# The last output tile in three pieces with its other terms summed ahead: a parallel attention and gated-MLP block

## The chip, the core and the metric

The kernel runs on one core of one Trainium2 chip. The metric is the device time of one execution in microseconds, as the median of several runs. The core has five engines with queues of their own: TensorE (PE) for matrix products, VectorE (DVE), ScalarE (ACT), GpSimd (POOL), and SyncE (SP), which here mostly issues DMAs. TensorE writes into PSUM, which VectorE and ScalarE read; DMAs move data between SBUF and the chip's memory. An engine works through its queue in order, and engines wait for each other by semaphores.

## What is computed

One block on a sequence of 2048 rows with 512 columns, in bfloat16. With `xn` the layer-normed input, the output is the residual plus two branches, both of which end in a matrix product:

```python
x = A_x                                   # (1, 2048, 512)
xn = _layernorm(x, axis=-1)
return x + _A_ref(xn, A_wqkv, A_wo) + _B_ref(xn, B_w_in, B_w_sp, B_b_sp, B_w_out)

# _A_ref: 32 heads of 16, each row attends to 8 rows behind it, 2 apart
#   o = softmax(q.k / 4) v ;  return o @ wo                   # (512 x 512)
# _B_ref: z = gelu(xn @ w_in);  z1, z2 = halves of 688
#   g = w_sp @ layernorm(z2) + b_sp                           # mixes the rows
#   return (z1 * g) @ w_out                                   # (688 x 512)
```

The "gated features" of the title are `z1 * g`; "the other part" is the attention branch and the last 48 of the 688 gated features.

## The kernel before, in words

The 2048 rows are 16 tiles of 128. Everything is written as named operations: `op_(name, after, f)` (line 149) stores a function and the names that must be issued before it. Five lists written out by hand (lines 569 to 616) give the order of the names on TensorE, ScalarE, VectorE, GpSimd and SyncE. `advance` (line 623) walks them, TensorE's list first, and issues what an operation needs ahead of it. The names in `after` only set the order of issue; the waits on the chip are added by the framework from the tiles that instructions read and write, and the traces show them per tile: who reads a PSUM tile waits for the last write that was issued into it, in whichever part of the tile.

The work goes through these stages: norm, transposes and the input products (lines 164 to 340), local attention on VectorE, the row mixing on TensorE (`mix`, line 467), the gate `z1 * g` on VectorE and its transposition by DMA into `uT` (line 474), and the output stage, which is where the change lies.

The output stage (lines 507 to 566) works on four groups of four tiles. Group n has tiles {0, 2, 4, 6}, {1, 3, 5, 7}, {8, 10, 12, 14} and {9, 11, 13, 15}. Each output tile (128 rows, 512 float32 columns) fills one PSUM bank. There are eight banks in five PSUM tiles: `mm[0]`, `mm[1]`, `mm[2]` with two banks each, `aux[0]`, `aux[1]` with one. Groups 0 and 2 use the first four entries of `banks` (lines 507 and 508), groups 1 and 3 the last four. Into each bank three products are summed:

- `gated_full` (line 512): 640 of the 688 gated features, five matmuls of 512 columns (`MF` is 5);
- `gated_rest` (line 517): the last 48 features, one matmul;
- `attention_out` (line 523): 64 narrow matmuls for the four tiles of a group side by side, one quarter of the array's rows each.

TensorE's list ends with `gf2 re2 re3 ao2 ao3` and then the full products of group 3, tile by tile. Group 3 thus has its short and its attention products first (`re3`, `ao3`), and its gated products last: tiles 9, 13 and 11 whole (`gf3.9`, `gf3.13`, `gf3.11`), tile 15 in two halves of 256 columns (`gfl0`, `gfl1`), both in the one bank `aux[1]`.

What follows a finished tile: for groups 0 and 1, ScalarE copies the bank (`E`, line 554) and VectorE adds the residual `xr` (`F`, line 555); for groups 2 and 3 VectorE adds the residual straight from PSUM (`F`, line 560) and writes bfloat16. SyncE stores the tile (`S`, line 561). Tile 15 has two adds of 256 columns (`Fl0`, `Fl1`, line 565) and two stores of 64 KB (`Sl0` from SyncE, `Sl1` from ScalarE, line 566). The residual `xr[1]` is loaded long before (`R1`, line 504).

`stmp` (line 85) is a float32 SBUF tile of 128 x 4 x 256 that the softmax uses (lines 394 to 404) and nothing after it. Line 664 is the end of the program: the last waits for all DMAs and the engines' closing handshake stand under it.

Of the kernel before, what the change touches and what calls it, by code (L numbers as in the profile page):

```python
# [10 lines left out]
ALU = mybir.AluOpType  # L11
PSUM = bass.MemoryType.PSUM

P = 128
S = 2048
D = 512
NT = S // P
C = D // P
DH = 16
# [8 lines left out]
F = 2 * FH  # L28
FHALF = FH // 2
MF = FH // P  # L30
# [12 lines left out]
def kernel(  # L43
# [13 lines left out]
    V = nc.vector  # L57
    A = nc.scalar
    G = nc.gpsimd
    PE = nc.tensor  # L60
    SP = nc.sync

    x2 = A_x.rearrange("b s d -> (b s) d")
    out2 = out.rearrange("b s d -> (b s) d")
# [20 lines left out]
    stmp = sb.tile([P, 4, GS], F32, name="stmp")  # L85
# [8 lines left out]
    wout = wts[:, DH * D:(DH + MF + 1) * D].rearrange("p (m n) -> p m n", m=MF + 1)  # L94
# [5 lines left out]
    uT = [r[:, 0:(MF + 1) * HS].rearrange("p (m s) -> p m s", m=MF + 1) for r in qk_r]  # L100
# [17 lines left out]
    xr = [wsp_r[n].rearrange("p (i d) -> p i d", i=8) for n in (2, 0)]  # L118
# [7 lines left out]
    mm = [ps.tile([P, 2, D], F32, name=f"mm{n}") for n in range(3)]  # L126
    aux = [ps.tile([P, D], F32, name=f"aux{n}") for n in range(2)]
# [21 lines left out]
    def op_(name, after, f):  # L149
        assert name not in do, name  # L150
        do[name], needs[name] = f, list(after)
# [146 lines left out]
    for i in range(NT):  # L298
        g = i // 4 * 4
# [73 lines left out]
    for c, th in BUF:  # L373
        n = f"{c}{th}"
# [128 lines left out]
    for th in range(2):  # L503
# [1 line left out]
            xr[th], x2[th * HS:(th + 1) * HS, :].rearrange("(i p) d -> p i d", p=P)))  # L505

    banks = [mm[0][:, 0, :], mm[0][:, 1, :], mm[1][:, 0, :], mm[1][:, 1, :],
             mm[2][:, 0, :], aux[0][:], mm[2][:, 1, :], aux[1][:]]
    groups = [[8 * th + 2 * g + t for g in range(4)] for th in range(2) for t in range(2)]
    po = {i: banks[4 * (n % 2) + g] for n, tiles in enumerate(groups) for g, i in enumerate(tiles)}  # L510

    def gated_full(i, start, stop, c=slice(0, D)):
        th, t0 = i // 8, (i % 8) * P
        for m in range(MF):
            PE.matmul(po[i][:, c], uT[th][:, m, t0:t0 + P], wout[:, m, c], start=(start and m == 0), stop=(stop and m == MF - 1))  # L515
# [7 lines left out]
    def attention_out(n, start, stop):  # L523
        th, s = n // 2, n % 2
        for d in range(DH):
            for g in range(4):
                PE.matmul(po[groups[n][g]], op[32 * g:32 * g + 32, th, d, s * P:(s + 1) * P], wo_r[32 * g:32 * g + 32, d, :],  # L527
                          start=(start and d == 0), stop=(stop and d == DH - 1), tile_position=(32 * g, 0))

    U = [[f"U{j}" for j in range(8 * th, 8 * th + 8)] for th in range(2)]  # L530
    EVM = [f"G{j}" for j in range(NT)] + ["Bc", "Tc4"]
    for n in (0, 1):
        op_(f"gf{n}", LO + U[0] + EVM, lambda n=n: [gated_full(i, True, False) for i in groups[n]])
        op_(f"re{n}", [f"gf{n}"], lambda n=n: gated_rest(groups[n], False, False))
        op_(f"ao{n}", [f"re{n}", "a0.11"], lambda n=n: attention_out(n, False, True))
    op_("gf2", U[1] + [f"E{i}" for i in groups[0]], lambda: [gated_full(i, True, False) for i in groups[2]])
    op_("re2", ["gf2"], lambda: gated_rest(groups[2], False, False))
    op_("re3", U[1] + [f"E{i}" for i in groups[1]], lambda: gated_rest(groups[3], True, False))
    op_("ao2", ["re2", "a1.11"], lambda: attention_out(2, False, True))
    op_("ao3", ["re3", "a1.11"], lambda: attention_out(3, False, False))  # L540
    halves = [slice(0, D // 2), slice(D // 2, D)]
    tail = [groups[3][g] for g in (0, 2, 1, 3)]
    for i in tail[:3]:
        op_(f"gf3.{i}", ["ao3"], lambda i=i: gated_full(i, False, True))
    for n, c in enumerate(halves):
        op_(f"gfl{n}", ["ao3"], lambda n=n, c=c: gated_full(groups[3][3], False, n == 1, c))

    def o_of(i):
        return ot[i]
# [10 lines left out]
                    lambda i=i: V.tensor_tensor(o_of(i), po[i], xr[1][:, i % 8, :], ALU.add))  # L560
            op_(f"S{i}", [f"F{i}"], lambda i=i: SP.dma_start(out2[i * P:(i + 1) * P, :], o_of(i)))

    for n, c in enumerate(halves):
        i = groups[3][3]
        op_(f"Fl{n}", [f"gfl{n}", "R1"], lambda c=c: V.tensor_tensor(o_of(i)[:, c], po[i][:, c], xr[1][:, i % 8, c], ALU.add))  # L565
        op_(f"Sl{n}", [f"Fl{n}"], lambda n=n, c=c: (SP, A)[n].dma_start(out2[i * P:(i + 1) * P, c], o_of(i)[:, c]))


    pe = """wu T0a T0 B wd z0a T1 z0b T2 z1 T3 z2 T4 z3 T5 z4 T6 z5 T7 z6 z7 y0 y1 z8 z9 z10 z11 z12 z13 z14
        k0 k1 q0 q1 z15 k2 k3 q2 q3 k4 k5 q4 q5 k6 k7 q6 q7  # L570
        v0 v1 v2 v3 v4 v5 v6 v7 y2 y3 y4 y5 y6 y7 y8 y9 y10 y11 y12 y13 y14 y15
        M0 M1 M2 M3 M4 M5 M6 M7 M8 M9 M10 M11 M12 M13 M14 M15
        gf0 gf1 re0 re1 ao0 ao1 gf2 re2 re3 ao2 ao3""".split() + [f"gf3.{i}" for i in tail[:3]] + ["gfl0", "gfl1"]
    for n in pe:
        a, x = n[0], n[1:]
        if n in do:
# [26 lines left out]
    dve = """b0 ag0 b1 ag1 n0a n0 b2 ag2 n1 b3 n2 ag3 b4 ag4 n3 b5 ag5 n4 b6 ag6 b7 n5""".split()  # L603
    for i in range(6, NT):
# [2 lines left out]
        m00 f00 p00 m01 zs8 m10 zb8 zs12 m11 p01 zb12 m20 p10 m21 p11 m30 p20 m31 p21 p30 X0 p31 HW u0 X1 C0 g0 a0.0 u1 a0.1 C1 g1 g2  # L607
        a0.2 g3 a0.3 g4 a0.4 g5 a0.5 a0.6 g6 a0.7 g7 a0.8 a0.9 g8 a0.10 a0.11 g9 g10 a1.0 a1.1 g11 a1.2 g12 a1.3 g13
        a1.4 g14 a1.5 a1.6 g15 a1.7 a1.8 a1.9 a1.10 a1.11""".split()
    OUT = [i for n in range(3) for i in groups[n]] + tail[:3]  # L610
    dve += [f"F{i}" for i in OUT] + ["Fl0", "Fl1"]
    pool = ["b16"] + [f"gr{i}" for i in range(NT)] + "zr0 zr4 f01 zr8 kh2 f10 zr12 kh3 f11 f20 f21 f30 f31".split()
    sp = """x0 x1 x2 x3 x4 x5 x6 x8 wy x12 wk wq wv t8 t9 t10 t11 t12 t13 t14 t15 W0 kh0 W1 kh1 vh
        W2 W3 LO0 LO1 W4 U0 W5 LO2 LO3 U1 U2 W6 LO4 U3 U4 W7 U5 U6 U7 U8 U9 U10 R0 U11 U12 U13 R1 U14 U15""".split()
    sp += [f"S{i}" for i in OUT] + ["Sl0"]
    act.append("Sl1")
    lists = [pe, act, dve, pool, sp]
    assert sorted(sum(lists, [])) == sorted(do), (set(do) ^ set(sum(lists, [])))
# [50 lines left out]
```

## Time and profile before

| | |
|---|---|
| runs | 200.99, 201.28, 201.07 us; median 201.07 |
| the profiled execution | 200.92 us |
| its span, first to last instruction | 199.1 us |
| granted TensorE clock | 1.0 |
| stores to the output | 15 of 128 KB and 2 of 64 KB |
| last matmul ends | 195.77 us in the span |
| last store issued | 196.58 us in the span |

All times inside an execution are counted from the start of the span. In the views, L515 is line 515 of the kernel; PE is TensorE's matmuls, PEld its weight loads, SPq and ACTq the DMA issues of SyncE and ScalarE. In a group's row, `out<-in` are the tiles, then come partitions x columns and types, the count, the busy time in us and the mean duration in ns, and then the idle time of the engine before it and who ended it. In the timeline a row that ends in x3 is three instructions run together: start of the first, time from there to the end of the last. A matmul's duration includes its way through the array, so durations of matmuls that follow each other overlap; adds of VectorE overlap by a little too.

### The profile page before, as it was taken

Reading aid. Unit: us, or ns where it says so; the run is one execution under the profiler, and the core shown is the slowest. Engines: PE = TensorE matmul, PEld = TensorE weight load, DVE = VectorE, ACT = ScalarE, POOL = GpSimd, SP = SyncE. Lnnn points to the kernel's source line nnn. Section 1 sums busy time; section 2 is a strip of 40 time slices with the busy share of each in tenths; the row PEclk is TensorE's granted clock in tenths of the full one; section 3 lists DMA queues with packets and bytes.
Section 4 is the critical chain, followed back from the end, with each engine's and each line's share of the span. In section 5 each row is a group of like instructions: output and inputs, shape, how many; then the busy total and the mean of one; then the engine's idle time right before and its main releaser. Section 6 shows DMA issues by size and latency. Waiting matters only on the chain.

```text
span 199.1 us, 4537 instructions
## 1 busy us (share of the span) xinstructions
PE 194.8 (98%) x1939; PEld 122.7 (62%) x1939; DVE 177.7 (89%) x203; ACT 89.8 (45%) x130; POOL 38.8 (19%) x67
## 2 busy tenths in 40 slices
PE   8999999999999999999999999999999999999993
PEld 2566666667777766666666666666666654443441
DVE  5999896899898999989999999999999999996234
ACT  2587898796559996671562211112211110043000
POOL 5577122002999330330000000000000000000000
PEclk9999999999999999999999999999999999999999
DMA  6999566910987999998199999999993569904133
GB/s 163 361 360 205 95 142 131 206 17 0 197 140 142 194 189 142 184 182 156 40 220 214 184 155 239 253 112 255 212 212 69 112 206 232 191 3 159 55 105 105
DMA packets 68452, 32.58 MB, mean 164 GB/s; under 512 B 56912, under 2 KB 66512, under 8 KB 68304
## 3 DMA queue, kind: packets, MB, share of 16 engines
q1 hardware_dynamic: 65568, 24.12, 58.8%
q0 software_dynamic: 2176, 7.40, 20.1%
q10 hardware_dynamic: 688, 0.77, 1.3%
q8 instruction: 15, 0.25, 0.5%
q14 instruction: 5, 0.04, 0.1%
HBM read 10.03 MB, written 2.10 MB: 61 GB/s over the span
## 4 chain that ended last, share of the span: by engine, by line
PE 94%; DMA 2%; DVE 1%; POOL 0%; SPq 0%; issue 0%; DVEq 0%
PE mm L471 37%; PE mm L321 21%; PE mm L230 18%; PE mm L527 7%; PE mm L515 7%; PE aux L515 2%; DMA z<-in_A_x_dram 2%; PE mm L520 1%; PE aux L212 1%; SPq L162 0%; DVE stats L169 0%; POOL rstd L176 0%; DVE z L565 0%; DVE z L179 0%; DVEq L664 0%
## 5 line engine op out<-in xcount | busy, mean ns | idle before, releaser
L471 PE MATMUL mm<-z,wsp 128*128 128x344 bf16 x512 | 74.8, 309 | 0.0
L471 PEld LDWEIGHTS <-wsp 128*128 128x128 bf16 x512 | 50.1, 98 | 24.6
L321 PE MATMUL mm<-xnT,wts 128*32 128x512 bf16 x768 | 41.9, 380 | 0.0
L230 PE MATMUL mm<-wts,xnT 128*128 128x344 bf16 x256 | 39.0, 309 | 0.0
L321 PEld LDWEIGHTS <-wts 128*32 128x32 bf16 x768 | 29.5, 140 | 12.0 <-issue 0.6
L422 DVE TENSOR_TENSOR prod<-vp,a_sb 128x4096 bf16<-128x4096 bf16 x16 | 36.1, 2285 | 0.0
L485 ACT ACTIVATE qk<-mm,b_col 128x688 bf16<-128x688 f32 x16 | 13.3, 831 | 46.0 <-PE mm L471 41.1
L230 PEld LDWEIGHTS <-xnT 128*128 128x128 bf16 x256 | 24.6, 98 | 12.1 <-issue 0.8
L355 DVE TENSOR_TENSOR prod<-qk 128x4096 bf16<-128x4096 bf16 x12 | 26.9, 2287 | 1.4 <-DMA qk<-qk 1.2
L426 DVE TENSOR_TENSOR prod<-prod,prod 128x8192 bf16<-128x8192 bf16 x6 | 26.5, 4420 | 0.0
L334 ACT CAST qk<-mm 128x1024 bf16<-128x1024 f32 x16 | 16.2, 1012 | 7.8 <-PE mm L321 7.8
L310 ACT ACTIVATE z<-mm 128x688 bf16<-128x688 f32 x16 | 11.8, 748 | 5.7 <-PE mm L230 5.3
L363 POOL DMA_DIRECT2D prod<-prod x10 | 8.7, 1022 | 27.9 <-DVE zvar L279 15.6
L527 PE MATMUL mm<-wts,xnT 32*128 32x512 bf16 x192 | 14.2, 374 | 0.0
L515 PEld LDWEIGHTS <-qk 128*128 128x128 bf16 x85 | 8.2, 98 | 9.4 <-issue 0.8
L515 PE MATMUL mm<-wts,qk 128*128 128x512 bf16 x60 | 13.6, 379 | 0.0
L247 ACT ACTIVATE z<-mm 128x688 bf16<-128x688 f32 x16 | 11.8, 744 | 1.8 <-PE mm L230 1.8
L169 DVE BATCH_NORM_STATS2 stats<-z 128x6 f32<-128x512 bf16 x16 | 10.7, 671 | 1.5 <-DMA z<-in_A_x_dram 1.4
L560 DVE TENSOR_TENSOR z<-mm,wsp 128x512 bf16<-128x512 f32 x6 | 3.8, 684 | 8.5 <-PE mm L527 5.2
L527 PEld LDWEIGHTS <-xnT 32*128 32x128 bf16 x256 | 6.4, 93 | 7.7 <-issue 0.8
L554 ACT CAST z<-mm 128x512 bf16<-128x512 f32 x6 | 3.2, 598 | 13.7 <-PE mm L527 12.3
L176 POOL TENSOR_TENSOR rstd<-rstd,mhalf 128x1 f32<-128x1 f32 x16 | 9.0, 561 | 1.3
(82 smaller groups left out, 170.2 us busy)
## 6 DMA issues: line engine op xcount, KB each, us to landing
prod<-prod POOLq DMA_DIRECT2D x10, 512.0 KB, 7.4
wts<-in_A_wo_dram SPq DMA_DIRECT2D x4, 512.0 KB, 6.6
wsp<-in_A_x_dram SPq DMA_DIRECT2D x2, 1024.0 KB, 6.0
out_dram<-z SPq DMA_DIRECT2D x15, 128.0 KB, 1.8
wts<-in_A_wqkv_dram SPq DMA_DIRECT2D x3, 512.0 KB, 8.6
z<-in_A_x_dram SPq DMA_DIRECT2D x2, 512.0 KB, 6.2
wsp<-z POOLq DMA_DIRECT2D x2, 512.0 KB, 6.4
wsp<-wts POOLq DMA_DIRECT2D x2, 512.0 KB, 8.8
```

The source lines that it names most:

```text
L230: PE.matmul(t[:, hh, 0:FHALF], xnT[:, kc, i * P:(i + 1) * P], w_z[part][:, kc, hh * FHALF:(hh + 1) * FHALF], start=(kc == 0), stop=(kc == ...
L247: A.activation(z2[:, i, :].rearrange("p (a b) -> p a b", a=2), t[:, :, 0:FHALF], ACT.Gelu_apprx_tanh, **total)
L310: op_(f"yg{i}", [f"y{i}"], lambda: A.activation(z1u[:, i, 0:FH].rearrange("p (a b) -> p a b", a=2), t[:, :, 0:FHALF], ACT.Gelu_apprx_tanh))
L321: PE.matmul(t[32 * g:32 * g + 32, dd, :], w, r, start=(kc == 0), stop=(kc == C - 1), tile_position=(0, 32 * g))
L334: op_(f"{a}c{p}", [f"{a}{p}"], lambda: A.copy(home(a, p), t[:].rearrange("p d (t s) -> p d t s", t=2)))
L355: V.tensor_tensor(pr, q, k, ALU.mult)
L422: return lambda: V.tensor_tensor(dst, vp[:, :, th, off:off + GS], a_sb[:, th, W - 1 - w].unsqueeze(1).broadcast_to([P, DH, GS]), ALU.mult)
L426: return lambda: V.tensor_tensor(dst, dst, x, ALU.add)
L471: PE.matmul(t[:, hh, 0:FHALF], w[:, k, (j % 2) * P:(j % 2 + 1) * P], z2[:, k, hh * FHALF:(hh + 1) * FHALF], start=(k == 0), stop=(k == NT ...
L485: lambda: A.activation(gs[j % 3].rearrange("p (a b) -> p a b", a=2), t[:, :, 0:FHALF], ACT.Identity, bias=b_col[:, j:j + 1]))
L515: PE.matmul(po[i][:, c], uT[th][:, m, t0:t0 + P], wout[:, m, c], start=(start and m == 0), stop=(stop and m == MF - 1))
L527: PE.matmul(po[groups[n][g]], op[32 * g:32 * g + 32, th, d, s * P:(s + 1) * P], wo_r[32 * g:32 * g + 32, d, :], start=(start and d == 0), ...
```

## The change

The last output tile, 15, no longer gathers all its terms in one bank.

- **Banks.** The last two entries of `banks` trade places: tiles 13 and 15 (and 5 and 7) trade `mm[2]`'s second half and `aux[1]`. Tile 15's short and attention products are now in `mm[2]`'s second bank; its accumulation ends with `ao3` (the `stop` flag).
- **Order.** Group 3's full products go 9, 11, 13 where they went 9, 13, 11.
- **The early sum.** `Fe`, a new VectorE add ahead of tile 9's, sums that bank and the residual into `early`, a float32 view of the first two quarters of `stmp`.
- **Three pieces.** Tile 15's gated product goes into three other banks: columns 0 to 255 into `mm[0]`, 256 to 383 into `mm[1]`, 384 to 511 into `aux[0]` (`last_full`: five matmuls each). `aux[0]` is the bank of tile 11, whose add must have read it.
- **Adds and stores.** `Fl0`, `Fl1`, `Fl2` add each piece to `early`; the stores are of 64, 32 and 32 KB from SyncE, ScalarE and SyncE.

```diff
     banks = [mm[0][:, 0, :], mm[0][:, 1, :], mm[1][:, 0, :], mm[1][:, 1, :],
-             mm[2][:, 0, :], aux[0][:], mm[2][:, 1, :], aux[1][:]]
+             mm[2][:, 0, :], aux[0][:], aux[1][:], mm[2][:, 1, :]]
...
                 PE.matmul(po[groups[n][g]], op[32 * g:32 * g + 32, th, d, s * P:(s + 1) * P], wo_r[32 * g:32 * g + 32, d, :],
-                          start=(start and d == 0), stop=(stop and d == DH - 1), tile_position=(32 * g, 0))
+                          start=(start and d == 0), stop=(d == DH - 1 and (stop or groups[n][g] == groups[3][3])), tile_position=(32 * g, 0))
...
-    halves = [slice(0, D // 2), slice(D // 2, D)]
-    tail = [groups[3][g] for g in (0, 2, 1, 3)]
-    for i in tail[:3]:
+
+    parts = [slice(0, D // 2), slice(D // 2, 3 * D // 4), slice(3 * D // 4, D)]
+    pieces = [(banks[n][:, 0:c.stop - c.start], c) for n, c in zip((0, 2, 5), parts)]
+    early = stmp[:, 0:2].rearrange("p a s -> p (a s)")
+    tail = [groups[3][g] for g in (0, 1, 2)]
+    for i in tail:
         op_(f"gf3.{i}", ["ao3"], lambda i=i: gated_full(i, False, True))
-    for n, c in enumerate(halves):
-        op_(f"gfl{n}", ["ao3"], lambda n=n, c=c: gated_full(groups[3][3], False, n == 1, c))
+    def last_full(t, c):
+        i = groups[3][3]
+        th, t0 = i // 8, (i % 8) * P
+        for m in range(MF):
+            PE.matmul(t, uT[th][:, m, t0:t0 + P], wout[:, m, c], start=(m == 0), stop=(m == MF - 1))
+
+    for n, (t, c) in enumerate(pieces):
+        op_(f"gfl{n}", ["Fe", f"F{tail[1]}"] + [f"F{i}" for i in groups[2]], lambda t=t, c=c: last_full(t, c))
...
-    for n, c in enumerate(halves):
-        i = groups[3][3]
-        op_(f"Fl{n}", [f"gfl{n}", "R1"], lambda c=c: V.tensor_tensor(o_of(i)[:, c], po[i][:, c], xr[1][:, i % 8, c], ALU.add))
-        op_(f"Sl{n}", [f"Fl{n}"], lambda n=n, c=c: (SP, A)[n].dma_start(out2[i * P:(i + 1) * P, c], o_of(i)[:, c]))
+    il = groups[3][3]
+    op_("Fe", ["ao3", "R1"], lambda: V.tensor_tensor(early, po[il], xr[1][:, il % 8, :], ALU.add))
+    for n, (t, c) in enumerate(pieces):
+        op_(f"Fl{n}", [f"gfl{n}", "Fe"], lambda t=t, c=c: V.tensor_tensor(o_of(il)[:, c], t, early[:, c], ALU.add))
+        op_(f"Sl{n}", [f"Fl{n}"], lambda n=n, c=c: (SP, A, SP)[n].dma_start(out2[il * P:(il + 1) * P, c], o_of(il)[:, c]))
...
-        gf0 gf1 re0 re1 ao0 ao1 gf2 re2 re3 ao2 ao3""".split() + [f"gf3.{i}" for i in tail[:3]] + ["gfl0", "gfl1"]
+        gf0 gf1 re0 re1 ao0 ao1 gf2 re2 re3 ao2 ao3""".split() + [f"gf3.{i}" for i in tail] + ["gfl0", "gfl1", "gfl2"]
...
-    OUT = [i for n in range(3) for i in groups[n]] + tail[:3]
-    dve += [f"F{i}" for i in OUT] + ["Fl0", "Fl1"]
+    OUT = [i for n in range(3) for i in groups[n]] + tail
+    dve += [f"F{i}" for i in OUT[:12]] + ["Fe"] + [f"F{i}" for i in OUT[12:]] + ["Fl0", "Fl1", "Fl2"]
...
-    sp += [f"S{i}" for i in OUT] + ["Sl0"]
+    sp += [f"S{i}" for i in OUT] + ["Sl0", "Sl2"]
     act.append("Sl1")
```

## The prediction

> **What bounds the kernel now.** I read the page first: what is busy over the whole span.
>
> ```profile
> span 199.1 us, 4537 instructions
> PE 194.8 (98%) x1939; PEld 122.7 (62%) x1939; DVE 177.7 (89%) x203; ACT 89.8 (45%) x130; POOL 38.8 (19%) x67
> PEclk9999999999999999999999999999999999999999
> ```
>
> TensorE is busy 98% of the span at full clock, so outside the end only fewer matmul cycles would help, and the change removes none: it computes the same columns in the same order of tiles. What is left is the last few microseconds. So I read the chain of waits in the window from 195 us on, then the timeline from 191.1 us.
>
> ```profile
> 194.99 0.78 PE aux L515 x7
> 195.77 0.02 issue
> 195.80 0.42 DVE z L565
> 196.22 0.33 DVEq L664
> ```
>
> The columns of both are start, duration (us), engine and line.
>
> ```profile
> 191.26 2.33 PE L515 MATMUL mm<-wts,qk 128*128 128x512 bf16 x10
> 193.42 2.33 PE L515 MATMUL aux<-wts,qk 128*128 128x512 bf16 x15
> 193.62 1.29 DVE L560 TENSOR_TENSOR z<-mm,wsp 128x512 bf16<-128x512 f32 x2 [3.23 <-PE mm L515]
> 194.34 1.53 SPq L561 DMA_DIRECT2D out_dram<-z  x3
> 194.83 0.68 DVE L560 TENSOR_TENSOR z<-aux,wsp 128x512 bf16<-128x512 f32 x1
> 195.80 0.76 DVE L565 TENSOR_TENSOR z<-aux,wsp 128x256 bf16<-128x256 f32 x2 [0.28 <-PE aux L515]
> 196.25 0.33 SPq L566 DMA_DIRECT2D out_dram<-z  x1
> 196.58 0.36 ACTq L566 DMA_DIRECT2D out_dram<-z  x1
> ```
>
> The last two stores by their source line, with the time from issue to landing:
>
> ```profile
> L566 SPq DMA_DIRECT2D out_dram<-z x1: 332/332/332, 196.2 to 196.2; - x1
> DMA to landing us min/median/max: 1.5/1.5/1.5
> L566 ACTq DMA_DIRECT2D out_dram<-z x1: 360/360/360, 196.6 to 196.6; - x1
> DMA to landing us min/median/max: 1.6/1.6/1.6
> ```
>
> The last matmul ends at 195.77. Only then, at 195.80, does VectorE start on the last tile, though its first half (`gfl0`) was complete five matmuls earlier: both halves are columns of one PSUM tile, and the first add waits for the whole tile. The same shows two rows up: the first add of the last group waits until 193.62, the end of all ten matmuls into `mm`, because tiles 9 and 13 share the PSUM tile `mm[2]`. Then 0.76 us for two adds, and the second store is issued by ACT at 196.58. It lands 1.6 us later, at about 198.18; the last 0.96 us to 199.14 are the kernel's closing steps, which the change leaves alone. The time between the last matmul and the last store's issue, 0.81 us, is what the change can shorten.
>
> **The change part by part.** Costs come from these rows.
>
> ```profile
> L515 PE MATMUL mm<-wts,qk 128*128 128x512 bf16 x60 | 13.6, 379 | 0.0
> L515 PE MATMUL aux<-wts,qk 128*128 128x256 bf16 x10 | 1.3, 272 | 0.0
> L515 PEld LDWEIGHTS <-qk 128*128 128x128 bf16 x85 | 8.2, 98 | 9.4 <-issue 0.8
> 14.92 0.39 PE L212 MATMUL aux<-ident,z 128*128 128x128 bf16 x4
> L212 PE MATMUL aux<-ident,z 128*128 128x128 bf16 x32 | 3.3, 221 | 0.2
> L560 DVE TENSOR_TENSOR z<-aux,wsp 128x512 bf16<-128x512 f32 x1 | 0.7, 681 | 0.0
> L399 DVE TENSOR_TENSOR stmp<-stmp 128x512 f32<-128x512 f32 x2 | 1.4, 692 | 0.1
> L565 DVE TENSOR_TENSOR z<-aux,wsp 128x256 bf16<-128x256 f32 x2 | 0.8, 420 | 0.3 <-PE aux L515 0.3
> L400 DVE TENSOR_TENSOR stmp<-stmp 128x256 f32<-128x256 f32 x2 | 0.9, 426 | 0.1
> ```
>
> *TensorE.* Ten matmuls span 2.33 us and the last lasts 0.38, so 512 columns go every 0.217 us. The three full tiles are now 9, 11, 13 and end at 192.51, 193.59 and 194.67; the first matmul of the last tile starts at 194.50 as before. 256 columns go every (195.77 - 194.50 - 0.27)/9 = 0.11. For 128 columns with a weight load each, the four transposes are the nearest row: (0.39 - 0.22)/3 = 0.057, although a load is 0.098 long. Piece 1 (five of 256) ends at 195.21, piece 2 (five of 128, from 195.05) at 195.50, piece 3 (from 195.33) at 195.78. So TensorE ends where it did; ten more narrow matmuls for five wide ones are free at this spacing. The new waits of these matmuls are for adds of tiles 10 and 14 (of the four below, all done by 190.4) and of tile 11 (done by 194.5, next paragraph): they are met long before, and the matmuls queued behind them do not stand.
>
> ```profile
> 180.39 0.62 ACT L554 CAST z<-aux 128x512 bf16<-128x512 f32 x1
> 187.91 2.48 DVE L560 TENSOR_TENSOR z<-mm,wsp 128x512 bf16<-128x512 f32 x4 [5.24 <-PE mm L527]
> ```
>
> *The early sum `Fe`.* It is one 512-column add from PSUM with a float32 result: the float32 rows (692 and 426) match those that write bfloat16 (681 and 420), so 0.69, and start to start 0.61 as in the pair of 1.29. It reads `mm[2]`, into which tile 9 is also written, and in the order of the changed kernel's instructions `Fe` names a wait for TensorE while tile 9's add behind it names none: one wait serves both, tile 9's end. So `Fe` starts at 192.54 in time when VectorE was idle (3.23 us before 193.62). Tile 9 follows at 193.15, tile 11 at 193.76 (ready 193.62), tile 13 at 194.70 (its matmuls end 194.67). The cover holds: `Fe` costs nothing unless it starts after 192.88.
>
> *The pieces.* VectorE is free again at 195.31; piece 1 was ready at 195.24, so it starts at 195.31 and piece 2 at 195.65 (0.34 later). Halving 512 to 256 columns took 0.27 off the spacing, so 128 columns take another 0.13 off: 0.21 start to start and 0.29 long. Piece 3 starts at 195.86 (ready 195.81) and ends at 196.15, where the second half ended at 196.56. VectorE, not TensorE, is what is late now, by 0.05.
>
> *The stores.* SP now issues tile 13's store, then pieces 1 and 3; ACT has piece 2. An issue follows an add's end by 0.03 (196.22 to 196.25). The price of stores that queue on SP is read where eight follow each other:
>
> ```profile
> 180.35 3.79 SPq L561 DMA_DIRECT2D out_dram<-z  x8
> L561 SPq DMA_DIRECT2D out_dram<-z x15: 332/392/804, 180.3 to 195.5; - x15
> DMA to landing us min/median/max: 1.7/1.8/2.2
> qk<-qk SPq DMA_DIRECT2D x2, 24.0 KB, 2.2
> ```
>
> (3.79 - 0.39)/7 = 0.49 apart, 0.09 more than an issue lasts. The stores at the end were issued in 0.33 each, so I take 0.42 here and keep 0.49 for the range. Tile 13's add ends at 195.38, its store is issued at 195.41; piece 1 was ready at 195.76 but goes at 195.83; piece 3 was ready at 196.18 and goes at 196.25. ACT issues piece 2 at 195.97, landing by 197.6: not last. So the last issue moves from 196.58 to 196.25, 0.33 earlier, and SP is by a little the tightest of the three engines.
>
> *The landing.* The last store now goes through SP: 1.5 instead of ACT's 1.6. It is 32 KB in rows of 256 bytes, which no row shows. The 128 KB stores take 1.8 (median) and 64 KB 1.5 to 1.6, so bytes alone would give 1.4; the nearest small pieces, the 24 KB halo copies in far more and shorter rows, took 2.2. I take 1.45, nearest to the output's own rows, and keep 1.4 and 2.2.
>
> The Trainium skill's page "DMA: Bandwidth & Descriptors", section Specifications, speaks against this: it asks for at least 512 bytes a piece and says that below it the engine does a read-modify-write. No run here shows such a store; by that rule the landing would lie nearer the upper end.
>
> *The new banks.* Tiles 5 and 7 and tiles 13 and 15 trade PSUM banks. All matmuls, copies and adds of those groups stay in number and length; ACT's last copy of the first of these groups ends at 181.01 (its row stands above), 10 us ahead of the tail. I cost this at nothing, its cover being TensorE's work until 191.
>
> *Sum.* 0.33 (issue) + 0.15 (landing 1.6 to 1.45) = 0.48 us off a span of 199.1. The profiled execution took 200.92 us, 1.8 outside its span; that becomes 200.44. The median of the three runs was 201.07, so 200.6.
>
> **The rivals.** A measurement here tells about 0.2%, 0.4 us, from no change, so a gain must exceed 0.4.
>
> 1. *Narrow matmuls go at the rate of their weight loads.* At 0.098 instead of 0.057, piece 3 starts its last matmul at 195.05 + 9 x 0.098 = 195.93 and ends at 196.15; its add ends at 196.47, the issue is at 196.50, landing 197.95: gain 0.23, 200.84. For it: a load is 0.098 long. Against it: the transposes, same load and same width, at 0.057. The Trainium skill's "TensorE: Matmul & The Clock Gate", section Back-to-back issue gap, gives 81 ns for 128 columns in a real stream and about 56 isolated; the trace agrees with the smaller figure. By 81 ns piece 3 would end at 196.00, the issue would be at 196.35 and the gain 0.38, an estimate.
>
> 2. *SP's queue and the short rows eat it.* With issues 0.49 apart the last goes at 196.39, and with a landing of 1.6 it is there at 197.99: gain 0.19, 200.88. At a landing of 2.2 from 196.25 it is 198.45, 0.27 later than now: 201.34, still within 0.2%. For it: the spacing is a row of the same kind of store, and the rows are the shortest ever written to the output. Against it: the stores of this stretch at 0.33.
>
> 3. *The pieces do not separate.* If all three adds still waited for the last matmul, 195.80 + 0.34 + 0.21 + 0.29 = 196.64 would put the issue at 196.67, with 1.45 to land: 198.12, 201.0. Against it: each of the three names its own wait for TensorE, on three PSUM tiles.
>
> 4. *Slower: SP's issues stretch.* One of the fifteen stores took 0.804 to issue. The place is SP, between tile 13's store at 195.41 and piece 3's. If these two issues took that, piece 3 would go at 195.41 + 2 x 0.89 = 197.19 and land at 198.64, 0.46 later than now: 201.5. It decides when the last issue falls after 198.18 - 1.45 = 196.73, that is from 0.66 between issues on. For it: three stores in a row where there were gaps of 0.6. Against it: one in fifteen, and not in this stretch.
>
> **How the numbers follow.** The forecast, pieces that separate with SP issuing about 0.42 apart: 70%. Its spread is about 0.3 to 0.65 us of gain: low when the landing stays at 1.5 and the runs scatter by 0.1; high when SP is no bound (196.18), the landing is 1.4 and the scatter helps. I put four fifths of it, 56%, beyond 0.4 and 14% within. Rival 1 has 8%, rival 2 has 11%, rival 3 has 4%, all within 0.2%; rival 4 has 7%. So faster 0.56, same 0.37, slower 0.07. The predicted time is the forecast's, 200.6. The range, 200.3 to 201.0, takes in the forecast's spread (200.4 to 200.8) with 0.1 us of scatter, rivals 1 and 3 and the milder half of 2; it leaves out rival 4, the long landing, and what is outside on both sides, under 2 in 10.
>
> **What would show it.** In the changed kernel's timeline: `Fe` near 192.54 and tile 9's add near 193.15 (if `Fe` starts with the third tile's end, its wait was read wrongly); the last add near 195.86, right behind the one before; ten matmuls of 128 columns within about 0.73 us of busy time (over 1.1: rival 1); tile 13's and pieces 1's and 3's stores on SP at 195.41, 195.83, 196.25 (0.49 apart or more: rivals 2 and 4); the landing of piece 3 in the list of DMA issues. The prediction is wrong if the span of the stages before 191 us changes: nothing in the change should reach there.

## The result and the profile after

Over 22 runs of each kernel, the median was 200.8 us (200.39 to 201.39) after the change and 201.25 us (200.82 to 201.58) before. The ratio is 0.9979, 95% interval 0.9971 to 0.9987: 0.13% to 0.29% faster, 0.42 us in the middle. That is clear of zero and right at the 0.2% that the prediction took as the line to "no change". The prediction said 0.48 us less (200.6, from a median of three runs of 201.07); the range 200.3 to 201.0 holds the result. Most of the 0.2 us between 200.6 and 200.8 is the starting point: the 22 runs of the kernel before have a median 0.18 us above that of the three.

The head of the page of the changed kernel:

```profile
span 199.1 us, 4552 instructions
PE 195.1 (98%) x1944; PEld 121.9 (61%) x1944; DVE 178.2 (90%) x205; ACT 89.6 (45%) x130; POOL 38.8 (19%) x67
PEclk9999999999999999999999999999999999999999
```

The span reads 199.1, as before. Whoever stopped here would say that nothing changed. The reason is a start that differs from one execution to the next. Here is the first group of transposes, first in the kernel before, then in the changed one (start, duration):

```profile
5.14 0.54 PE L212 MATMUL aux<-ident,z 128*128 128x128 bf16 x4
```

```profile
5.28 0.65 PE L212 MATMUL aux<-ident,z 128*128 128x128 bf16 x4
```

After 8 us the changed kernel's execution is 0.39 us behind, and TensorE stays 0.37 to 0.39 behind through every stage up to the last group of tiles (VectorE is up to 0.87 behind from 89 us on, where it waits for a DMA, without holding TensorE up). The order of work is the same on every engine up to the trade of banks at 168.6 us, so nothing that the change touches lies there. The prediction had called itself wrong if the stages before 191 us changed, so this needs an answer: in the nine profiles used below, whose kernels differ only in the output stage, TensorE's first weight load of the last group starts between 191.25 and 191.67 and its last matmul ends between 195.76 and 196.19. The lag lies within this scatter, and the 22 runs of each kernel show the gain that the ends show, without the lag. So the ends of the kernels are compared here **from the end of TensorE's last matmul**: 195.76 before, 196.14 after. The timeline of the changed kernel's end:

```profile
191.63 1.25 PE L515 MATMUL mm<-wts,qk 128*128 128x512 bf16 x5
192.72 2.32 PE L515 MATMUL aux<-wts,qk 128*128 128x512 bf16 x10
192.92 0.69 DVE L573 TENSOR_TENSOR stmp<-mm,wsp 128x512 f32<-128x512 f32 x1 [2.16 <-PE mm L515]
193.53 0.68 DVE L569 TENSOR_TENSOR z<-mm,wsp 128x512 bf16<-128x512 f32 x1
194.12 0.68 DVE L569 TENSOR_TENSOR z<-aux,wsp 128x512 bf16<-128x512 f32 x1
194.88 0.99 PE L552 MATMUL mm<-wts,qk 128*128 128x256 bf16 x10
195.08 0.69 DVE L569 TENSOR_TENSOR z<-aux,wsp 128x512 bf16<-128x512 f32 x1 [0.27 <-PE aux L515]
195.68 0.61 DVE L575 TENSOR_TENSOR z<-mm,stmp 128x256 bf16<-128x256 f32 x2
195.70 0.44 PE L552 MATMUL aux<-wts,qk 128*128 128x128 bf16 x5
195.79 0.33 SPq L570 DMA_DIRECT2D out_dram<-z  x1
196.21 0.28 DVE L575 TENSOR_TENSOR z<-aux,stmp 128x128 bf16<-128x128 f32 x1
196.22 0.88 SPq L576 DMA_DIRECT2D out_dram<-z  x2
196.32 0.37 ACTq L576 DMA_DIRECT2D out_dram<-z  x1
196.70 0.40 SPq L576 DMA_DIRECT2D out_dram<-z  x1
```

The rows of single SP issues, at 195.79 (tile 13's store) and in the last row (piece 3's, the second of the two SP issues two rows above), were asked for alone. Three things are to be seen. The first two pieces' adds begin at 195.68, while TensorE is still at work until 196.14: the wait for the whole last tile is gone. The adds of tile 13 and of the pieces follow each other without a gap, so VectorE has taken TensorE's place, by little: its last add starts 0.07 us after TensorE's end, and e2 below has an add that waited for TensorE start 0.04 after it. And VectorE's last add ends at 196.49, but SP issues its store only at 196.70: SP is still busy with the store before. From TensorE's end, the last store is issued at 0.56, where it was 0.82, and the span ends at 2.98, where it was 3.38: **0.39 us less**, within the measured interval (0.26 to 0.58 us).

The landing times of the last three stores, the last row that of piece 3 (the two halves had 1.5 on SP and 1.6 on ACT). Piece 2's, on ACT, took 1.7 and landed 0.19 us before piece 3's:

```profile
out_dram<-z SPq DMA_DIRECT2D x1, 64.0 KB, 1.6
out_dram<-z ACTq DMA_DIRECT2D x1, 32.0 KB, 1.7
out_dram<-z SPq DMA_DIRECT2D x1, 32.0 KB, 1.5
```

### The profile page after: what moved, and what is told of

The parts are those of the page before. It is cut to its first block, busy times and chain, and to the rows that moved or that the text cites. A ratio compares the mean times of both kernels' runs of the same rounds, so it can differ in the third digit from the quotient of the medians.

```text
span 199.1 us, 4552 instructions
## 1 busy us (share of the span) xinstructions
PE 195.1 (98%) x1944; PEld 121.9 (61%) x1944; DVE 178.2 (90%) x205; ACT 89.6 (45%) x130; POOL 38.8 (19%) x67
## 4 chain that ended last, share of the span: by engine, by line
PE 94%; DMA 3%; issue 1%; SPq 1%; DVE 1%; DVEq 0%
PE mm L471 37%; PE mm L321 21%; PE mm L230 18%; PE mm L527 7%; PE mm L515 6%; DMA z<-in_A_x_dram 3%; PE aux L515 2%; PE aux L212 1%; PE mm L520 1%; SPq L162 1%; DVE z L575 0%; PE aux L520 0%; DVE z L179 0%; PE aux L527 0%; DVEq L674 0%
## 5 line engine op out<-in xcount | busy, mean ns | idle before, releaser
L321 PEld LDWEIGHTS <-wts 128*32 128x32 bf16 x768 | 28.4, 139 | 13.2 <-issue 0.6
L515 PEld LDWEIGHTS <-qk 128*128 128x128 bf16 x75 | 7.2, 98 | 9.1 <-issue 0.8
L515 PE MATMUL mm<-wts,qk 128*128 128x512 bf16 x55 | 12.5, 379 | 0.0
L334 ACT CAST vp<-mm 128x1024 bf16<-128x1024 f32 x8 | 8.1, 1016 | 0.7 <-PE mm L321 0.7
```

What stands on the lines that cost most here:

```text
L321: PE.matmul(t[32 * g:32 * g + 32, dd, :], w, r, start=(kc == 0), stop=(kc == C - 1), tile_position=(0, 32 * g))
L334: op_(f"{a}c{p}", [f"{a}{p}"], lambda: A.copy(home(a, p), t[:].rearrange("p d (t s) -> p d t s", t=2)))
```

## The experiments

The theory to test: the gain comes from the pieces' own PSUM tiles, which let the first adds start before TensorE ends; what is left at the end is set by SP's queue of stores. The rivals: the early sum and the order make the gain; the small last piece makes it; the stores' bytes and short rows set the end. The runs of one kernel lie 0.7 to 2.7 us apart from the lowest to the highest (e4, with four runs, 0.1), so differences under 0.2 us are read in the traces, and each trace is one execution.

| run | ratio to before (95%) | median less before's | last issue | end of span |
|---|---|---|---|---|
| before | 1 | 0 | 0.82 | 3.38 |
| changed | 0.9979 (0.9971 to 0.9987) | -0.45 | 0.56 | 2.98 |
| e1, tile 13's store on ACT | 0.9974 (0.9955 to 0.9993) | -0.57 | 0.41 | 2.92 |
| e2, two pieces | 0.9963 (0.9936 to 0.9991) | -0.47 | 0.49 | 3.04 |
| e3, two pieces, one tile | 1.0000 (0.9979 to 1.0020) | -0.10 | 0.83 | 3.38 |
| e4, banks and order only | 1.0074 (1.0049 to 1.0099) | +1.66 | 2.62 | 5.17 |
| e5, merged store on ACT | 0.9979 (0.9960 to 0.9998) | -0.46 | 0.38 | 2.93 |
| e6, merged store on SP | 0.9999 (0.9974 to 1.0024) | -0.27 | 0.56 | 3.13 |
| e7, early sum late | 1.0011 (0.9996 to 1.0025) | +0.22 | 1.20 | 3.62 |

All but the ratios are us. The last two columns are counted from the end of TensorE's last matmul, in the profiled execution. The ratio is not the quotient of the two medians, and in e2 and e6 the two differ by over 0.1%; in each run the difference of the medians follows the end of the span to 0.15 us.

**e3: is it the tiles of their own?** Two pieces in the two halves of one bank, early sum and order kept:

```diff
-    pieces = [(banks[n][:, 0:c.stop - c.start], c) for n, c in zip((0, 2, 5), parts)]
+    pieces = [(banks[0][:, c], c) for c in parts]
     # not shown: parts has two slices of 256 columns; the third piece's add and store are gone
```

> The changed kernel with two pieces of 256 columns in the two halves of one PSUM tile (one bank), with the early sum kept and stores from SP and ACT. Theory: the gain is from pieces in PSUM tiles of their own, since an add waits for the last write into its tile. Then both adds wait for TensorE's end again: counted from the first full matmul of the last group, the first starts at 4.54, the last store is issued at 5.32 as in the kernel before, and the ratio is 1.000. Rival: the gain is from the early sum and the new order, which keep VectorE free at the end; then the last issue is at about 5.0 and the ratio 0.998.

```profile
194.55 1.25 PE L552 MATMUL mm<-wts,qk 128*128 128x256 bf16 x10
194.75 0.69 DVE L569 TENSOR_TENSOR z<-aux,wsp 128x512 bf16<-128x512 f32 x1 [0.27 <-PE aux L515]
195.84 0.76 DVE L575 TENSOR_TENSOR z<-mm,stmp 128x256 bf16<-128x256 f32 x2 [0.40 <-PE mm L552]
196.63 0.37 ACTq L576 DMA_DIRECT2D out_dram<-z  x1
```

VectorE was free from 195.44 and stood for 0.40 us until TensorE's end at 195.80, although the first half was whole long before. The whole gain is gone: end 3.38, ratio 1.0000. So the early sum and the new order by themselves bring nothing; the pieces' own PSUM tiles bring it. The run e2 below is the closest pair: its two pieces of 256 columns differ from these only in the PSUM tiles, and its end is at 3.04.

**e4: banks and order without the rest.** The kernel before, with two edits:

```diff
-             mm[2][:, 0, :], aux[0][:], mm[2][:, 1, :], aux[1][:]]
+             mm[2][:, 0, :], aux[0][:], aux[1][:], mm[2][:, 1, :]]
-    tail = [groups[3][g] for g in (0, 2, 1, 3)]
+    tail = [groups[3][g] for g in (0, 1, 2, 3)]
```

> The kernel before with only the trade of the two banks and the order 9, 11, 13: tile 15's halves are in the PSUM tile that also holds tile 9. Theory (an add waits for the last write issued into its PSUM tile, and the adds are issued after all matmuls): tile 9's add waits for the very last matmul, and tiles 11 and 13 stand behind it on VectorE; three adds of 0.61 go behind TensorE's end, the last issue moves from 5.32 to about 7.15, and the time is 1.8 us (0.9%) longer. Rival (waits go by bank): the time stays within 0.1%.

```profile
194.64 1.25 PE L515 MATMUL mm<-wts,qk 128*128 128x256 bf16 x10
195.93 0.69 DVE L560 TENSOR_TENSOR z<-mm,wsp 128x512 bf16<-128x512 f32 x1 [5.41 <-PE mm L515]
196.54 1.28 DVE L560 TENSOR_TENSOR z<-aux,wsp 128x512 bf16<-128x512 f32 x2
197.74 0.75 DVE L565 TENSOR_TENSOR z<-mm,wsp 128x256 bf16<-128x256 f32 x2
198.51 0.36 ACTq L566 DMA_DIRECT2D out_dram<-z  x1
```

VectorE stands idle for 5.41 us, to the end of all matmuls, while one tile after another is finished: tile 9's add is held, and those of 11 and 13 stand behind it. The end moved by 1.79 us, as worked out. Tiles 9 and 15 have different banks here, so the wait goes by the PSUM tile and not by the bank. The trade of banks is harmless in the changed kernel because tile 15's last matmuls go to other tiles: nothing is written into `mm[2]` after tile 9's matmuls.

**e7: the early sum where nothing hides it.**

```diff
-    dve += [f"F{i}" for i in OUT[:12]] + ["Fe"] + [f"F{i}" for i in OUT[12:]] + ["Fl0", "Fl1", "Fl2"]
+    dve += [f"F{i}" for i in OUT] + ["Fe", "Fl0", "Fl1", "Fl2"]
```

> The changed kernel with the early sum moved behind tile 13's add on VectorE, so that it is no longer hidden. Theory: the early sum costs 0.61 us of VectorE and was free only in the idle time before tile 9. Counted from the first full matmul of the last group, tile 13's add still starts near 3.45, the sum at 4.05, the first piece at 4.66, the third at 5.19, the last store is issued at 5.50 to 5.55: the end 0.45 us later than the changed kernel's, 0.05 to 0.1 later than before's, ratio 1.000. Rival: VectorE has slack there and SP is the only bound; then the end is later by under 0.3.

```profile
195.12 0.69 DVE L569 TENSOR_TENSOR z<-aux,wsp 128x512 bf16<-128x512 f32 x1 [0.39 <-PE aux L515]
195.73 0.68 DVE L573 TENSOR_TENSOR stmp<-mm,wsp 128x512 f32<-128x512 f32 x1
196.51 0.62 DVE L575 TENSOR_TENSOR z<-mm,stmp 128x256 bf16<-128x256 f32 x2
196.97 0.81 SPq L576 DMA_DIRECT2D out_dram<-z  x2
```

The end is 0.63 us later than the changed kernel's, more than the 0.45 expected. The sum itself goes 0.61 after tile 13's add, as it should. But the first piece, which reads the sum, starts 0.79 after it and not 0.61: this add needs the one just ahead and started 0.1 after its end (195.73 + 0.68 = 196.41), while an independent add overlaps with the one ahead of it. The kernel before has such a pair too, in the softmax, where the second add reads what the first wrote:

```profile
98.47 0.69 DVE L399 TENSOR_TENSOR stmp<-stmp 128x512 f32<-128x512 f32 x1
99.20 0.43 DVE L400 TENSOR_TENSOR stmp<-stmp 128x256 f32<-128x256 f32 x1
```

There, too, the second does not start before the first has ended. So the cover that the early sum has in the changed kernel is worth 0.63 us, more than the whole gain, and the size in the expectation was off by this 0.18.

**e2: what is the third piece worth?** Two pieces of 256 columns, in `mm[0]` and `mm[1]`, stored by SP and ACT:

```diff
-    parts = [slice(0, D // 2), slice(D // 2, 3 * D // 4), slice(3 * D // 4, D)]
+    parts = [slice(0, D // 2), slice(D // 2, D)]
     # not shown: the third piece's product, add and store are gone from the lists
```

> The changed kernel with two pieces of 256 columns, in two PSUM tiles, stored by SP and ACT with 64 KB each. Theory: what the change gains is that the first piece's add no longer waits for the last matmul; the third piece gives almost nothing, because SP loses what VectorE gains. Counted from the first full matmul of the last group, the second add starts at 4.54 (TensorE's end), ends at 4.96, ACT issues at 4.99, landing 1.6: the end within 0.05 us of the changed kernel's, ratio 0.998. Rival: the smaller last piece is what gains (VectorE 0.28 instead of 0.42 after the last matmul); then the end is 0.14 or more later than the changed kernel's.

```profile
194.68 1.25 PE L552 MATMUL mm<-wts,qk 128*128 128x256 bf16 x10
195.48 0.91 DVE L575 TENSOR_TENSOR z<-mm,stmp 128x256 bf16<-128x256 f32 x2
196.02 0.38 SPq L576 DMA_DIRECT2D out_dram<-z  x1
196.42 0.36 ACTq L576 DMA_DIRECT2D out_dram<-z  x1
```

The end is at 3.04, 0.06 later than with three pieces and 0.34 earlier than before. The expectation had 0.05 as the most. The last store is even issued sooner (0.49 instead of 0.56); it took 0.06 longer to land, and the closing steps behind it 0.07 longer (told of below). Two pieces thus have most of the gain, as the theory had it; the ratios of the two cannot be told apart.

**e1 and e5: SP's queue relieved.** e1 issues tile 13's store from ACT. e5 stores pieces 2 and 3 together from ACT, after piece 3's add.

```diff
# e1
-            op_(f"S{i}", [f"F{i}"], lambda i=i: SP.dma_start(...))
+            op_(f"S{i}", [f"F{i}"], lambda i=i: (A if i == tail[2] else SP).dma_start(...))
# e5 (Sl1 is the only store on ACT's list, Sl2 is gone)
-        op_(f"Sl{n}", [f"Fl{n}"], lambda n=n, c=c: (SP, A, SP)[n].dma_start(...))
+    for n, m, e, c in ((0, 0, SP, slice(0, D // 2)), (1, 2, A, slice(D // 2, D))):
+        op_(f"Sl{n}", [f"Fl{m}"], lambda e=e, c=c: e.dma_start(out2[il * P:(il + 1) * P, c], o_of(il)[:, c]))
```

> The changed kernel with one edit: tile 13's store is issued by ACT, so SP has only pieces 1 and 3 at the end. Times are counted from the first full matmul of the last group (191.63 in the changed kernel, whose last store is issued 5.07 after it). Theory: SP's queue sets the last issue, VectorE's last add being done 0.18 earlier. Then piece 1 goes at 4.50, piece 3 at 4.89 to 4.92, and the end comes 0.15 to 0.18 earlier than in the changed kernel: about 0.6 us (0.3%) under the kernel before. Rival: the stores share the DMA engines, and the last landing is set by the bytes ahead of it and by its short rows. Then the issue moves but the landing takes that much longer (1.7 instead of 1.5), and the ratio stays at the changed kernel's 0.998.

```profile
195.56 0.44 PE L552 MATMUL aux<-wts,qk 128*128 128x128 bf16 x5
196.07 0.28 DVE L575 TENSOR_TENSOR z<-aux,stmp 128x128 bf16<-128x128 f32 x1
196.19 0.36 ACTq L576 DMA_DIRECT2D out_dram<-z  x1
196.41 0.40 SPq L576 DMA_DIRECT2D out_dram<-z  x1
```

> The changed kernel with three pieces, but pieces 2 and 3 stored together (64 KB, rows of 512 bytes) by ACT after piece 3's add. Theory (SP's queue sets the last issue): ACT is free, so the issue follows the add's end at 4.86 by 0.03, 4.89 after the first full matmul of the last group, with ACT's landing of 1.6: the end is 0.05 to 0.15 us earlier than the changed kernel's. Rival (short rows cost in landing): more than that, 0.2 or above, since no row is under 512 bytes any more.

```profile
195.54 0.44 PE L552 MATMUL aux<-wts,qk 128*128 128x128 bf16 x5
196.06 0.28 DVE L575 TENSOR_TENSOR z<-aux,stmp 128x128 bf16<-128x128 f32 x1
196.37 0.36 ACTq L577 DMA_DIRECT2D out_dram<-z  x1
```

In both the last store follows VectorE's last add (ends 196.35 and 196.34) by 0.03 to 0.06, where it was 0.21 in the changed kernel. So the lateness of the issue was SP's queue. But of e1's 0.15 us only 0.06 came to the end, where the theory had 0.15 to 0.18: its last store took 1.62 from issue to the wait that it ended, against 1.53 in the changed kernel. So the rival's longer landing came, by 0.09 of its 0.2. Its reason did not, as the trace's records of single DMA packets show: the packets of this store moved from 0.92 to 1.17 us after the issue, in the changed kernel from 0.90 to 1.17. The landing followed the last of them by 0.43 us instead of 0.35. In e1 the last four stores (256 KB) are issued within 0.75 us, from 195.66, and in the changed kernel within 0.91; whether that delays the landing, no run shows alone. e5 gained 0.05, its lower bound. Both are on the good side of the changed kernel by their traces, and neither is told apart from it by its ratio; there is little left here.

**e6: the price of the short rows.** As e5, with the merged store from SP, in the place of the changed kernel's last store on SP and at the same moment (0.56). What varies is not the rows alone: the store has twice the bytes too, and ACT's store just ahead is gone.

```diff
-    ... ((0, 0, SP, slice(0, D // 2)), (1, 2, A, slice(D // 2, D))):
+    ... ((0, 0, SP, slice(0, D // 2)), (1, 2, SP, slice(D // 2, D))):
```

> As the run before, but the merged store is issued by SP, in the place of piece 3's store: same queue, same number of stores ahead of it, same moment (5.07 after the first full matmul of the last group), 64 KB in rows of 512 bytes instead of 32 KB in rows of 256. It measures what the short rows cost. Theory: fixed costs dominate, the landing stays at 1.5 to 1.6, the end within 0.1 us of the changed kernel's, later if anything. Rival: rows under 512 bytes are dearer; then this lands earlier than the 1.5 of the changed kernel's last store.

From the list of DMA issues at its end:

```profile
out_dram<-z SPq DMA_DIRECT2D x3, 128.0 KB, 1.7
out_dram<-z SPq DMA_DIRECT2D x2, 64.0 KB, 1.6
```

64 KB in rows of 512 bytes landed in 1.61, 32 KB in rows of 256 bytes in 1.53 (issue to the end of SP's wait for it). Rows of half the length brought no penalty that outweighs the half of the bytes. Whether a smaller one hides behind the bytes, the packets tell: in the tails of the changed kernel, e6 and e7 a packet of 256 bytes took 18 ns in the median, one of 512 bytes 27 and one of 1024 bytes 46 to 47. Eight packets for each of the 16 DMA engines, 9 ns dearer, make 0.07 of the 0.08 us. ACT's queue (q10) shows the same where its one store was of 64 KB (e2) and where it was of 32 KB (e7), as packets, MB and share of the engines' time from 185 us on:

```profile
q10 hardware_dynamic: 144, 0.07, 1.3%
q10 hardware_dynamic: 144, 0.03, 0.9%
```

So a short row is dearer per byte but cheaper as a row. The end is 0.15 later than the changed kernel's, outside the expected 0.1: 0.08 from the landing, 0.07 from the order of SP's closing waits, which is told of below.

## Why the prediction was right

- *What bounds the end*: right. The add that waits for a whole PSUM tile was the place, shown by e3 (take the tiles away and all is as before) and e4 (put the wrong tile there and 1.79 us are lost).
- *TensorE*: right. (The order of tiles is not the same, as the prediction says at its start: 11 and 13 trade places. It costs nothing, as every full tile has five equal matmuls.) Ten matmuls of 128 columns with a load each go 0.055 us apart (0.44 for five, the last 0.22 long: 0.22/4); rival 1, the rate of the loads at 0.098, is out. By this the isolated gap, about 56 ns, that the Trainium skill's "TensorE: Matmul & The Clock Gate", section Back-to-back issue gap, gives holds here, and its 81 ns for a real stream does not.
- *The early sum*: right that it is free where it stands, as it starts in VectorE's idle time (192.92, right after tile 9's end) and tile 9's add follows by 0.61. e7 shows the price without cover.
- *The pieces*: right to 0.02 us. From the first full matmul of the last group the four adds of tile 13 and the pieces were predicted at 3.44, 4.05, 4.39 and 4.60, and started at 3.45, 4.06, 4.39 and 4.59.
- *The stores*: **the step that was mis-sized.** SP is the tightest, as said, but I took 0.42 between issues, with 0.49 kept for the range. The issue behind tile 13's came 0.42 later, the one behind that 0.49 later, because the issue ahead of it took 0.39 instead of 0.33. The 0.33 was read from stores that followed a pause; the row 332/392/804 held the other size. The last issue moved by 0.26 and not by 0.33.
- *The landing*: also too large. Issue to the end of SP's wait was 1.59 on ACT before and 1.53 on SP after: 0.06, not 0.15. Most of the term was the printed difference of 1.5 and 1.6, which is rounded, and a guess for fewer bytes. The long landing of rival 2 did not come on SP, and piece 2's store, with the same short rows, took 1.7 on ACT without being last. The rule of the Trainium skill's "DMA: Bandwidth & Descriptors", section Specifications (at least 512 bytes for line rate, below that a read-modify-write), shows no step at 512 here: packets of 256, 512 and 1024 bytes took 18, 27 and 46 to 47 ns, so bytes move the slower the shorter the packet, and 32 KB still cost less than 64.
- *The closing steps*: "the change leaves alone" was wrong by 0.07, to the good. From the end of the wait for the last store to the end of the span it was 0.96 before and 0.89 after.

The sum as measured in the traces: 0.26 + 0.06 + 0.07 = 0.39 us for 0.48. The two terms of the prediction came to 0.32 together, and the 0.07 that brought the sum nearer was foreseen by nobody: that part is luck. Rival 3 (pieces that do not separate) and rival 4 (SP's issues at 0.80) are out; rival 2's packed spacing came true for one of two issues. The 0.21% that came lies on the line that split the forecast's chance into 0.56 beyond and 0.14 within.

## What to carry to other kernels

At the end of a kernel, find what the last add waits for: if it is a tile that is still written in another part, give the last part a tile of its own, and sum whatever is ready ahead in the engine's idle time. The gain ends where the next queue begins, here the issues of the stores, so count what each queue has to issue in the last microsecond and spread it before cutting the work finer: two pieces had most of what three had. And compare tails from a mark near the end, not spans, when the start scatters by as much as the effect.

## What had not been expected of the hardware

- An issue on SP that stands right behind another took 0.38 to 0.40 us in these tails (0.392 and 0.395 in the changed kernel, 0.400 in e1), the first after a pause 0.33.
- An add on VectorE that reads the result of the add just ahead started 0.79 us after it, and an independent one 0.61 (each behind an add of 512 columns, e7). The dependent pair of the softmax is 0.73 apart, 0.03 behind the first one's end; the add in e7, 0.1 behind the end, waits for a product of TensorE as well as for the sum.
- Most of a small store's landing is not its data: of the 1.52 us of the changed kernel's last store (32 KB), 0.90 passed before its first packet and 0.35 after its last; the packets took 0.27.
- SyncE's closing waits for the DMAs stand in a fixed order, about 0.06 us apart when they need not wait. Where the last store to land was also the last one waited for, 0.89 us passed to the end of the span (changed kernel, e1, e7); where another wait stood behind it, 0.95 to 0.96 (before, e2 to e6).
